# State in 1 KB rows, half of the first x in fp32 by hardware queues, identity transposes ahead of early matmuls, and softmax and w2 work moved to GpSimd

## The chip, the cores and the metric

The kernel runs on one core of a Trainium2 chip. Its engines work side by side: TensorE (PE in the profile, its weight loads PEld), VectorE (DVE), ScalarE (ACT), GpSimd (POOL) and SyncE (SP), which here only issues transfers. The metric is the time of one execution on the device in microseconds (us); lower is better.

## The reference

Two stages follow each other. The first is a cross attention between tokens and a small state, in both directions; the second sends every row through all eight experts, weighted by a matrix that Sinkhorn iterations make.

```python
# x: (8, 8, 512, 64), state: (8, 8, 32, 64)
scores = scale * x @ state^T;   a  = softmax(scores);   xread = a @ state
scores2 = scale * state @ x^T;  a2 = softmax(scores2);  sread = a2 @ x
x = concat([xread, sread], axis=2) -> (4352, 512)       # B*S rows, H*D columns
P = exp(x @ w_gate - max)                               # (4352, 8)
for _ in range(8):
    P /= P.sum(1) + 1e-9;  P /= P.sum(0) + 1e-9;  P *= N / E
for e in range(8):                                      # w1: (512, 1024), w2: (1024, 512)
    out += P[:, e:e+1] * (relu(x @ w1[e]) @ w2[e])
```

## The kernel before

The attention is cut into 16 units, (b, q): batch b and half q of its heads, four heads each. For a unit, x (`x_nat`, cast to fp16 by GpSimd's software queue while it is loaded) is transposed to `xT`: for b < 2 by TensorE (line 578), for the others by a transposing DMA on SP's queue (line 591). `psB` holds the scores of both directions, made of `xT` and the transposed state `stT` (line 605). From there two chains go:

- the token softmax (names with A): DVE turns the scores into `eA`, takes the maximum, subtracts it (`subA`, line 648), ACT takes the exponential, DVE the sum and its reciprocal, DVE or POOL normalizes (`normA`, line 670), and DVE transposes the result to `aT`. The two units of batch 0 (`TOK = 2`) take their scores from TensorE in the token layout instead (`psA`, with `stD`, a spread copy of `stT`), and are transposed back by TensorE (`aT_ps`);
- the state softmax (names with B): maximum on DVE, exponential `E` with its row sum on ACT, reciprocal on DVE, scaling by it (`normB`, line 662) on POOL or DVE, a transposing DMA to `ETs`, and products `su_ps` with `x_nat` (line 758), which also set x buffers free.

xread is never formed. The state is multiplied into the weights first: `V = state @ w1` (`project`, `v_ps`, line 870), and the hidden layer of a batch is `hps = V^T aT` (line 897), then relu. The second layer is `yps` (line 935) for expert 0, and a scheme with fewer products (seven instead of eight, with sums of hidden rows `sm` and of weights `T`) for experts 1 to 7 (`layer1`, `layer2`, lines 255 and 334). The sums `T` of w2 of expert 1 are eight DVE subtractions (line 965) in the stretch of the Sinkhorn iterations.

Three things overlap in the first 134 us: the 16 attention units, expert 0 block by block as units become ready, and, after the last gate, eight Sinkhorn iterations on DVE, each with one column sum on TensorE (`csb_ps`, line 846). Products of expert 0 fill TensorE meanwhile. From 134 us on come experts 1 to 7, issued by loops; `layer2_last` computes the last 256 rows and stores them with eight transfers of 64 KB, alternating between SP's and ACT's queues (line 317).

The order of everything before expert 1 is written out by hand: the program makes a list of operations, each with the engines it may run on, and `PLAN` names number and engine of one after another, as in `662P` or `648A` (P is TensorE, V DVE, A ACT, G POOL, S SP's queue, H the host). Each engine runs its own in that order; the costs in the code beside an operation, such as `{"PE": (0.44, 0.62)}`, are not used by `issue`.

At the start, state is loaded by SP and ACT in two transfers (line 441) of 256 KB each, in rows of 256 bytes, cast and doubled to `st_in` by two engines, and transposed to `stT` by TensorE (line 492). POOL's queue loads x, then the halves of w1 and w2 of expert 0 (lines 468, 545, 548).

Of the kernel before, what the change touches and what calls it, by code (L numbers as in the profile page):

```python
# [12 lines left out]
ALU = mybir.AluOpType  # L13
# [3 lines left out]
6G 0S 1S 2V 7H 44V 3A 33V 32A 34A 8G 56P 36P 35V 55H 37V 10H 45V 57A 42P 58V 9G 38P 40P 43A 59P 4S 39A 41V 5V  # L17
46V 62P 50H 51G 61A 71V 63P 60A 52G 64V 11G 72V 73A 80P 65V 12G 435P 401P 66A 81V 13H 79P 14G 82V 436A 88V
437A 404P 83A 67V 402A 137H 403A 89V 96H 97P 100P 84V 406A 68V 90A 98A 15G 85V 69P 86P 53G 405A 99V 87V 70A
103P 101A 102A 91V 409P 16H 92G 413P 104V 407P 410A 411P 105V 111A 438P 120P 414V 408A 419P 421P 106V 415P  # L20
112V 138S 121V 74V 439A 412A 422V 113V 417P 107A 54G 440A 75G 122V 432P 429P 123V 370V 420A 469P 128A 418A
416A 17G 108V 140P 124A 125V 423P 426P 471A 433P 114A 148V 93S 129V 430P 149V 172H 424P 76S 434A 115V 470A
109G 130V 139S 110V 126G 141V 131A 427P 18G 127V 142V 428V 431A 445P 143V 132V 94P 150A 95V 77P 425A 156P 116G
447P 151V 133V 78V 449P 446A 443P 441P 144A 455P 164V 152G 448A 117S 19H 450V 157V 444A 165V 173S 442A 451P
456A 166A 134S 20G 452A 453P 463P 158V 472P 207H 145V 175P 159V 183V 184V 457P 31G 146G 454A 176V 473A 160A
464P 185A 174S 460P 458P 461P 465A 147V 161V 21G 153S 177V 191P 47P 162G 474A 118P 167V 459A 154P 462A 178V
163V 135P 49A 168G 199V 22H 48V 179A 466P 136A 352P 475P 200V 192V 201A 193V 119V 467P 476A 194V 23G 195A 485P
202V 208S 210P 180V 169S 155A 218V 356P 353A 481P 357V 468A 487P 219V 24G 489P 181G 186V 211V 242H 486A 482A
477P 490V 488A 483P 479P 220A 170P 478A 503P 187G 480A 484V 171A 203G 196V 537P 209S 25H 212V 226P 197G 504A
505A 506P 213V 500P 182V 198V 26G 234V 221V 507A 222V 204S 188S 491P 27G 538A 227V 539A 501P 497P 502A 508A  # L30
492P 235V 243S 228V 244S 214A 229V 511P 215V 236A 523P 230A 498P 494P 216G 245P 495P 515P 512V 499A 277H 231V
524A 493A 517P 246V 253V 223S 496A 247V 521P 516A 237V 254V 519P 509P 522V 518A 248V 513P 232G 189P 520A 255A
205P 510V 224P 514V 540P 28H 278S 261P 249A 190V 269V 29G 225A 270V 262V 531P 534P 206V 238G 250V 532P 256V
358P 271A 535P 217V 541A 533A 233V 542A 312H 279S 263V 272V 536A 354P 280P 528P 543P 529P 525P 288V 289V 251G
555P 264V 281V 265A 282V 239S 257V 526P 359A 266V 544A 530V 556A 545P 355A 547P 549P 273G 553P 527A 546V 571P
313S 290A 548A 283V 605P 550A 554V 296P 267G 606V 304V 572A 305V 240P 573A 557P 284A 607A 558A 551P 297V 552A
568P 360P 258S 241V 285V 30G 291V 306A 559P 562P 574P 298V 252V 315P 299V 286V 569P 576A 268V 323V 563P 575A
274S 300A 560P 570A 292G 316V 361A 561A 581P 564A 307V 565P 362P 324V 317V 301V 325A 302G 566P 363V 582A 326V
579P 587P 583P 287V 314S 588V 591P 567A 580A 639P 608P 584A 592A 347H 303V 331P 577P 348G 641V 640A 610A 609A
339V 293S 589P 585P 275P 332V 259P 578A 327G 586A 260A 590A 294P 340V 308G 333V 341A 593P 309S 318V 319A 334V  # L40
295V 364P 594P 276V 328S 625P 619P 342V 595A 335A 365A 599P 320V 602P 343V 336V 600P 337V 603P 626A 321G 322V
329P 310P 350G 344S 601A 349G 311A 620V 345P 338V 346V 604V 366P 596P 330A 368P 369V 351G 597P 367A 371V 611P
372P 598A 695H 615P 617P 373V 612V 374P 375V 613P 614V 616A 623P 618A 621P 696H 711H 376A 705P 377V 642P 624A
622A 706A 707A 630P 643V 697V 708P 644A 378P 379V 631P 710A 627P 698V 380V 647P 632A 709A 636P 628P 381P 633P
699V 648V 637P 382V 634P 657P 629A 638A 383V 700V 653P 658A 655P 384P 651P 635A 701V 654A 725P 385V 723P 386V
702V 656A 726A 716P 652A 724A 717A 645P 659P 649P 714P 646A 650A 660A 387P 721P 715A 712P 727P 687P 722A 388V
728A 688A 667P 713A 664P 389V 390P 703V 665P 668P 391V 673P 674A 392V 661P 670P 669A 729V 393P 671P 394V 666A
662P 672A 677P 395V 718P 663A 678A 679P 675P 683P 719A 681P 720V 680A 676A 685P 396P 684A 682A 397V 686A 692P
704V 689P 693P 690P 730P 398V 694A 399P 733P 731V 691A 732A 735A 734A 400V
""".split()  # L50
ENGINES = {"P": "PE", "V": "DVE", "A": "ACT", "G": "POOL", "D": "DMA", "S": "SPQ", "H": "HOST"}
NT_ = 2
ETX = 0
POOLB = 1
# [50 lines left out]
def issue(ops):  # L105
    for step in PLAN:
        op = ops[int(step[:-1])]
        assert all(d.end for d in op.after) and ENGINES[step[-1]] in op.on
        for slot in op.takes:
            slot.ring.taken.append(slot)  # L110
            slot.tile = slot.make()
        op.emit(ENGINES[step[-1]])
        op.end = True
    assert all(op.end for op in ops) and len(PLAN) == len(ops)
# [3 lines left out]
def kernel(  # L118
# [180 lines left out]
    def layer2_last():  # L299
# [5 lines left out]
        for row in range(tn // 128):  # L305
# [10 lines left out]
            for i in range(nb):  # L316
                (nc.scalar if i % 2 else nc.sync).dma_start(
                    out=outs[row * nb + i], in_=acc[ds(i * Ns, Ns), k, :])
# [116 lines left out]
    st_in = spl.tile([128, B, NQ, 2, D], FP16, name="st_in")  # L435
    st_st = spl.tile([128, B, NQ, D], FP32, name="st_st")
    loads = []
    for g in range(2):
        def load(g=g):
            bs = ds(g * B // 2, B // 2)  # L440
            (nc.scalar if g else nc.sync).dma_start(
                out=st_st[:, bs], in_=state[bs].rearrange("b (q h) n d -> (h n) b q d", q=NQ))

        loads.append(dma((0, 0), 1.0, load, lands=2.7))
        ops[-1].since, ops[-1].hard = 0.5, 1
# [5 lines left out]
    wgd = dma((0, 2), 0.1, lambda: nc.sync.dma_start(  # L451
        out=wg_st, in_=moe_w_gate.rearrange("(kc p) e -> p kc e", p=128)))
    wgc = op((15.0,), {"DVE": (0.15, 0.25)}, lambda _: nc.vector.tensor_copy(out=wgh, in_=wg_st), [wgd])
    wgc.since = 20.0
# [7 lines left out]
    for b in range(B):  # L462
        x_ready.append([])
        part("x%d" % b)
        got = op((0, 1 + 2 * b), {"HOST": (0.0, 0.0)}, lambda _: None, takes=[xn[b]])
        for g in range(2):
            def load(b=b, g=g):
                nc.gpsimd.dma_start(
                    out=xn[b].tile[:, ds(g * 4, 4), :],
                    in_=x[b, ds(g * 4, 4), :, :].rearrange("h (p sc) d -> p h (sc d)", sc=NSC))  # L470

            x_ready[b].append(dma((0, 1 + 2 * b, g), 1.28 if b else 2.3 - 0.6 * g, load, [got], [], [xn[b]], "POOL"))
            ops[-1].since, ops[-1].hard = 0.7, 1
# [4 lines left out]
    bd = []  # L478
    for g in range(2):
        for s_ in range(2):  # L480
            def place(eng, g=g, s_=s_):
                bs = ds(g * B // 2, B // 2)
                copy(eng, st_in[:, bs, :, s_, :], st_st[:, bs])

            bd.append(op((0, 0, g), {"DVE": (0.50, 0.64)} if s_ else {"ACT": (0.50, 0.65)}, place, loads[g:g + 1] + warmed))
    stT_ready = []
    for g in range(4):
        ps = psum([128, 4, 128], FP16, "stT_ps")

        def turn(_, g=g, ps=ps):  # L490
            for i in range(4):
                nc.tensor.transpose(ps.tile[:, i], st_in[:, 2 * g + i // 2, i % 2].rearrange("p s d -> p (s d)"),
                                    identh)

        def keep(eng, g=g, ps=ps):
            copy(eng, stT[:, ds(2 * g, 2)].rearrange("p b q c -> p (b q) c"), ps.tile)

        t = op((0, 1, g), {"PE": (0.35, 0.55)}, turn, bd[g // 2 * 2:g // 2 * 2 + 2] + [makeh], [ps])
        stT_ready.append(op((0, 1, g), EVICT16, keep, [t], uses=[ps]))
    ND = (TOK + 1) // 2  # L500
    stD_ready = {}
    if TOK:
        stD = spl.tile([128, ND, NQ, 4, 2, Ns], FP16, name="stD")
        zd = op((0, 0, 0), {"POOL": (0.40, 0.50), "DVE": (0.25, 0.35)}, lambda eng: engines[eng].memset(stD, 0.0))
        for b in range(ND):
            def spread(eng, s_, b=b):
# [4 lines left out]
                               lambda eng, s_=s_, spread=spread: spread(eng, s_), stT_ready[b // 2:b // 2 + 1] + [zd])  # L511
# [55 lines left out]
    for b in range(B):  # L567
# [4 lines left out]
                  [x_ready[b][0]], [xT])  # L572
        for g in range(2 if b < NT else 0):
# [11 lines left out]
            t = op((due_x(2 * b + g) - 2.0, 0), {"PE": (0.70, 0.88)}, turnX, [x_ready[b][g], makeh], [ps], [xn[b]])  # L585
# [3 lines left out]
        for g in range(0 if b < NT else 2):  # L589
# [5 lines left out]
            xt_ready.append([dma((due_x(2 * b - 2), 0, g), 2.0, turn, [x_ready[b][g], gotT], [], [xn[b], xT], lands=0.8)])  # L595
            ops[-1].moves, ops[-1].xbar = (3.0, 0.8), 1
            ops[-1].on = {"SPQ": (1.4, 4.5)}
        for q in range(NQ):
# [18 lines left out]
            o2 = op((due_x(2 * b + q), 0), {"PE": (0.13, 0.38)}, score, xt_ready[q] + stT_ready,  # L617
# [490 lines left out]
```

## Time and profile before

| | |
|---|---|
| median of 3 runs | 754.57 us (753.24 to 755.26) |
| the profiled execution | 753.05 us |
| its span, first to last instruction | 751.3 us |
| mean granted TensorE clock | 0.997 |
| start of the first hidden product of expert 0 | 18.66 us |
| start of the first product of expert 1 | 134.45 us |
| end of the last accumulation on DVE | 747.81 us |

In the profile, a line of a group or of the rows in order of time names the line of the kernel, the engine, the operation, what it writes and reads (out<-in), the shapes, and how often; idle time of the engine ahead of it stands in brackets, with what ended it. The mean of a matmul's duration includes its way through the array, so eight in a row take less than eight times the mean. The chain of waits goes back from the last instruction to what released it, step by step. The clock is given as a share of full speed.

### The profile page before, as it was taken

Reading aid. Unit: us, or ns where it says so; the run is one execution under the profiler, and the core shown is the slowest. Engines: PE = TensorE matmul, PEld = TensorE weight load, DVE = VectorE, ACT = ScalarE, POOL = GpSimd, SP = SyncE. Lnnn points to the kernel's source line nnn. Section 1 sums busy time; section 2 is a strip of 40 time slices with the busy share of each in tenths; the row PEclk is TensorE's granted clock in tenths of the full one; section 3 lists DMA queues with packets and bytes.
Section 4 is the critical chain, followed back from the end, with each engine's and each line's share of the span. In section 5 each row is a group of like instructions: output and inputs, shape, how many; then the busy total and the mean of one; then the engine's idle time right before and its main releaser. Section 6 shows DMA issues by size and latency. Waiting matters only on the chain.

```text
span 751.3 us, 16144 instructions
## 1 busy us (share of the span) xinstructions
PE 734.7 (98%) x6517; PEld 501.2 (67%) x6517; DVE 616.3 (82%) x1529; ACT 518.2 (69%) x1014; POOL 70.8 (9%) x81
## 2 busy tenths in 40 slices
PE   4999999999999999999999999999999999999997
PEld 3444445667677777777777677776777777776776
DVE  5999989888888789788887888887897888878875
ACT  6876846798976766666666766667667666676662
POOL 3664310200010000100000000100001000000000
PEclk9999999999999999999999999999999999999999
DMA  9997560600032000600006000330006000002234
GB/s 175 151 133 127 86 92 1 113 2 1 1 66 48 2 1 2 113 1 1 2 4 110 2 1 1 58 56 1 1 2 112 2 1 2 1 29 101 98 113 141
DMA packets 51323, 36.71 MB, mean 49 GB/s; under 512 B 25392, under 2 KB 43824, under 8 KB 51248
## 3 DMA queue, kind: packets, MB, share of 16 engines
q0 software_dynamic: 22272, 20.97, 18.4%
q1 hardware_dynamic: 27744, 14.18, 7.7%
q8 instruction: 51, 0.84, 0.5%
q10 hardware_dynamic: 1232, 0.52, 0.3%
q14 instruction: 24, 0.20, 0.1%
HBM read 42.48 MB, written 8.91 MB: 68 GB/s over the span
## 4 chain that ended last, share of the span: by engine, by line
PE 91%; DVE 3%; DMA 2%; ACT 1%; POOL 1%; issue 0%; SPq 0%; POOLq 0%; ACTq 0%
PE hps L255 28%; PE Bseed L334 20%; PE A L334 14%; PE E L334 13%; PE yps L935 6%; PE v_ps L235 4%; PE hps L897 4%; DMA xT<-x_nat 2%; DMA x_nat<-in_x_dram 1%; DVE acc L348 1%; ACT Hm L275 1%; PE su_ps L758 0%; PE y L312 0%; PE v_ps L870 0%; POOL E L662 0%; ACT V L419 0%
## 5 line engine op out<-in xcount | busy, mean ns | idle before, releaser
L275 ACT ACTIVATE Hm<-hps 128x512 f16<-128x512 f32 (+1 forms) x496 | 265.2, 577 | 128.1 <-PE hps L255 125.3
L255 PE MATMUL hps<-aT,V 128*128 128x512 f16 x880 | 230.1, 379 | 0.0
L334 PEld LDWEIGHTS <-Hm 128*128 128x128 f16 x1888 | 181.4, 98 | 71.2 <-issue 15.8
L348 DVE SCALAR_TENSOR_TENSOR acc<-Bseed,Pmat,acc 128x256 f32<-128x256 f32 x354 | 155.0, 477 | 9.4 <-PE Bseed L334 6.6
L334 PEld LDWEIGHTS <-sm 128*128 128x128 f16 x1416 | 138.2, 98 | 34.1 <-issue 0.4
L334 PE MATMUL A<-w2h,Hm 128*128 128x256 f16 x944 | 123.7, 273 | 0.0
L334 PE MATMUL Bseed<-T,Hm 128*128 128x256 f16 x944 | 123.3, 273 | 0.0
L255 PEld LDWEIGHTS <-V 128*128 128x128 f16 x880 | 86.1, 98 | 51.3
L348 DVE SCALAR_TENSOR_TENSOR acc<-E,Pmat,acc 128x256 f32<-128x256 f32 x236 | 103.1, 476 | 12.5 <-PE E L334 12.5
L281 DVE TENSOR_TENSOR sm<-Hm 128x512 f16<-128x512 f16 (+1 forms) x122 | 50.1, 411 | 64.2 <-ACT Hm L275 64.0
L243 ACT CAST V<-v_ps 128x512 f16<-128x512 f32 x150 | 77.7, 611 | 0.0
L348 DVE SCALAR_TENSOR_TENSOR acc<-A,Pmat,acc 128x256 f32<-128x256 f32 x118 | 51.9, 479 | 17.2 <-PE A L334 16.7
L935 PE MATMUL yps<-w2h,hT 128*128 128x512 f16 x272 | 64.1, 379 | 0.0
L363 ACT COPY Bseed<-A 128x512 f32<-128x512 f32 (+1 forms) x62 | 34.1, 550 | 43.3 <-PE A L334 42.1
L334 PE MATMUL E<-T,sm 128*128 128x256 f16 x472 | 61.7, 273 | 0.0
L334 PE MATMUL E<-w2h,sm 128*128 128x256 f16 x472 | 61.7, 273 | 0.0
L334 PE MATMUL Bseed<-T,sm 128*128 128x256 f16 x472 | 61.5, 272 | 0.0
L282 DVE TENSOR_TENSOR Hm<-Hm 128x512 f16<-128x512 f16 (+1 forms) x122 | 50.2, 412 | 4.2
L284 DVE TENSOR_TENSOR sm<-Hm,sm 128x512 f16<-128x512 f16 (+1 forms) x122 | 50.2, 412 | 4.2
L283 DVE TENSOR_TENSOR sm<-sm,Hm 128x512 f16<-128x512 f16 (+1 forms) x122 | 49.4, 405 | 0.0
L194 POOL DMA_DIRECT2D w1h<-in_moe_w_dram x12 | 8.5, 714 | 397.9 <-PE hps L255 397.4
L935 PEld LDWEIGHTS <-hT 128*128 128x128 f16 x272 | 25.4, 99 | 28.8 <-issue 1.7
(127 smaller groups left out, 609.7 us busy)
## 6 DMA issues: line engine op xcount, KB each, us to landing
w1h<-in_moe_w_dram POOLq DMA_DIRECT2D x16, 512.0 KB, 7.0
w2h<-in_moe_w_dram POOLq DMA_DIRECT2D x16, 512.0 KB, 8.1
out_dram<-acc SPq DMA_DIRECT2D x32, 256.0 KB, 2.6
x_nat<-in_x_dram POOLq DMA_DIRECT2D x16, 256.0 KB, 5.6
st_st<-in_state_dram ACTq DMA_DIRECT2D x1, 256.0 KB, 4.9
st_st<-in_state_dram SPq DMA_DIRECT2D x1, 256.0 KB, 4.3
ETs<-E SPq DMA_TRANSPOSE x16, 3.9
out_dram<-acc SPq DMA_DIRECT2D x4, 64.0 KB, 1.7
```

Source lines behind the costliest of these rows:

```text
L235: nc.tensor.matmul(ps[q][ds(j * Ns, Ns), :], stT[ds(r, 64), bi, q, ds((j ^ q) * Ns, Ns)], w1h[ds(r, 64), 2 * q + j // 2, cols], tile_posit ...
L243: nc.scalar.copy(out=dst, in_=src)
L255: nc.tensor.matmul(out, lhs, rhs, start=(k == 0), stop=(k == len(terms) - 1))
L275: nc.scalar.activation(out=Hm[:, i, j, :tn], in_=hps[:, :tn], func=AF.Relu)
L281: nc.vector.tensor_add(s1, a21, a22)
L282: nc.vector.tensor_sub(a21, a11, a21)
L283: nc.vector.tensor_sub(s2, s1, a11)
L284: nc.vector.tensor_sub(s4, a12, s2)
L334: nc.tensor.matmul(dst[:, c], lhs(j, c), rhs[:, j], start=first and c == 0 and j == 0, stop=(j == NJ - 1), skip_group_check=True)
L348: nc.vector.scalar_tensor_tensor(out=dst, in0=src[:, c], scalar=p[:, k], in1=dst, op0=ALU.mult, op1=ALU.add)
L363: nc.scalar.copy(out=Bb[:, :nk], in_=A[:, :nk])
L935: nc.tensor.matmul(yps.tile, hT[fb].tile[:, ds(tk * 128, 128)], w2h[:, fb, :], start=(fb == 0), stop=(fb == NFB - 1))
```

## The change

The edit has these parts:

1. `state` is read as rows of 1 KB (four state rows of 64 floats side by side in a partition), 128 KB first and then 384 KB in one transfer, both by SP. Four casts with a broadcast make `st_in`, one for each two batches, alternating between engines; the copy out of `stT_ps` puts the columns back in order. Users of `stT` wait for the quarter that they read, not for all four.
2. Heads 0 to 3 of batch 0 are loaded as fp32 by SP and ACT, 256 KB each, into a part of `acc` that is not in use yet, and cast to `x_nat` by DVE and ACT. POOL's software queue loads heads 4 to 7 and all other batches. `wg_st` is loaded later.
3. `IDLE` names seven operations of TensorE ahead of which 2 to 24 transposes (or products) of the identity with itself are issued, 72 in all, into the PSUM tile that the operation then overwrites.
4. `subA` and the sums `T` of expert 1 may run on POOL; `normB` on POOL is a product of two tensors, with the reciprocal broadcast, instead of a tensor times a scalar.
5. `layer2_last` stores its two row tiles with one transfer (256 KB, SP) and two (128 KB each, SP and ACT).
6. `PLAN` is another order of the same operations, with other engines for some. In it ten of the 14 subtractions of `subA` are on POOL (none before), 13 of 16 scalings `normB` (12 before), 9 of 16 normalizations (12 before), and four of the eight sums `T`. Nothing is edited in the loops of experts 1 to 7.

```diff
@@ issue @@
-def issue(ops):
+def issue(ops, idle):
     for step in PLAN:
...
+        idle(op.takes[0].tile if op.takes else None, IDLE.get(int(step[:-1]), 0))
         op.emit(ENGINES[step[-1]])
...
+IDLE = {34: 24, 59: 2, 62: 5, 404: 9, 106: 24, 407: 6, 37: 2}
...
+    def idle(t, n):
+        if not n:
+            return
...
+        for _ in range(n):
+            if t.dtype == FP16:
+                nc.tensor.transpose(t, identh, identh)
+            else:
+                nc.tensor.matmul(t, identh, identh, start=True, stop=True, skip_group_check=True)
@@ layer2_last @@
-            for i in range(nb):
-                (nc.scalar if i % 2 else nc.sync).dma_start(
-                    out=outs[row * nb + i], in_=acc[ds(i * Ns, Ns), k, :])
+                (nc.scalar if c else nc.sync).dma_start(
+                    out=outs[ds(row * nb, nb), :, cols], in_=acc[:, k, cols])
@@ the loads of state and x @@
-            (nc.scalar if g else nc.sync).dma_start(
-                out=st_st[:, bs], in_=state[bs].rearrange("b (q h) n d -> (h n) b q d", q=NQ))
+    st_rows = state.rearrange("b h (k l) d -> (b h k) (l d)", l=4).rearrange("(g p) c -> p g c", p=128)
+    xs = acc[:, ds(0, 2 * XH), :].rearrange("p (g t) d -> p g (t d)", t=2)
...
+        return begin("SPQ", lambda: nc.sync.dma_start(out=st_st[:, a:b], in_=st_rows[:, a:b]), 0.35 * (b - a))
...
+        q = nc.scalar if k else nc.sync
+        return begin("ACT" if k else "SPQ", lambda: q.dma_start(
+            out=xs[:, g, ds(k * 512, 512)].rearrange("p (h c) -> p h c", h=2),
+            in_=x[0, ds(4 * g + 2 * k, 2)].rearrange("h (p sc) d -> p h (sc d)", sc=NSC)), 0.68)
+    loads = load_st(0, 1)
+    xs_in = [[load_x(g, k) for k in range(2)] for g in range(XH)]
+    loads += load_st(1, B // 2) * 3
...
+                    copy(eng, xn[0].tile[:, ds(4 * g + 2 * k, 2), :].rearrange("p h c -> p (h c)"),
+                         xs[:, g, ds(k * 512, 512)])
@@ state to stT @@
+            copy(eng, st_in[:, g], st_st[:, g].rearrange("p (l d) -> p l d", d=D).unsqueeze(2)
+                 .broadcast_to((128, 4, 2, D)))
...
-            copy(eng, stT[:, ds(2 * g, 2)].rearrange("p b q c -> p (b q) c"), ps.tile)
+            copy(eng, stT[:, ds(2 * g, 2)].rearrange("p b q (m l) -> p (b q m) l", l=4), ps.tile.rearrange("p (l m) -> p m l", l=4))
@@ softmax and sums @@
-                engines[eng].tensor_scalar(out=E2.tile, in0=E2.tile, scalar1=rrec.tile, scalar2=None,
-                                           op0=ALU.mult)
+                if eng == "POOL":
+                    nc.gpsimd.tensor_mul(E2.tile, E2.tile, rrec.tile.broadcast_to((128, S)))
+                else:
+                    nc.vector.tensor_scalar(out=E2.tile, in0=E2.tile, scalar1=rrec.tile, scalar2=None, op0=ALU.mult)
...
-                s1 = op(r(4), {"DVE": (0.60, 0.80)}, subA, [m1], [], [eA, mxA])
+                s1 = op(r(4), {"DVE": (0.60, 0.80), "POOL": (1.05, 1.20)}, subA, [m1], [], [eA, mxA])
...
-        nc.vector.tensor_sub(T[:, i, jj], p[:, jj], q[:, jj])
+        engines[eng].tensor_sub(T[:, i, jj], p[:, jj], q[:, jj])
```

## The prediction

> **What bounds the kernel now.** I read the page first, then the busy time by stretch, then the rows of TensorE (PE) in order of time, then the rows of the softmax tiles. The page:
>
> ```profile
> span 751.3 us, 16144 instructions
> ...
> PE 734.7 (98%) x6517; PEld 501.2 (67%) x6517; DVE 616.3 (82%) x1529; ACT 518.2 (69%) x1014; POOL 70.8 (9%) x81
> ...
> PE 91%; DVE 3%; DMA 2%; ACT 1%; POOL 1%; issue 0%; SPq 0%; POOLq 0%; ACTq 0%
> ```
>
> PE sets the time, so only microseconds in which PE waits or runs slowly can be gained. The busy time by stretch says where those are:
>
> ```profile
> core 0: us, PE busy (x) PEld busy (x) DVE busy (x) ACT busy (x) POOL busy (x), PEclk, DMA share, GB/s
> 0.00:7.00 7.00, 0.02 (x1) 0.02 (x2) 1.47 (x4) 2.64 (x4) 6.25 (x14) 1.00 0.88 137
> 7.00:15.00 8.00, 6.18 (x91) 4.60 (x92) 5.98 (x14) 5.49 (x12) 1.26 (x2) 1.00 1.30 197
> 15.00:20.00 5.00, 3.97 (x36) 2.17 (x35) 4.62 (x12) 4.87 (x12) 1.04 (x1) 0.68 1.38 201
> 20.00:100.00 80.00, 77.76 (x883) 36.59 (x882) 73.21 (x165) 60.89 (x137) 42.86 (x41) 1.00 0.84 122
> 100.00:134.40 34.40, 34.13 (x216) 17.21 (x213) 30.64 (x84) 21.71 (x45) 0.00 (x0) 1.00 0.19 32
> 134.40:747.00 612.60, 612.38 (x5305) 440.61 (x5298) 499.89 (x1252) 422.63 (x808) 19.35 (x25) 1.00 0.17 36
> 747.00:751.30 4.30, 0.29 (x3) 0.01 (x1) 0.48 (x1) 0.00 (x0) 0.00 (x0) 0.93 0.49 122
> ```
>
> Experts 1 to 7 (134.4 to 747) have no PE idle time and are not edited. What can be won lies in the first 20 us, in 2.2 us of idle time between 20 and 100, and behind 747. PE's own rows:
>
> ```profile
> 6.98 1.04 PE L578 MATMUL xT_ps<-identh,x_nat 128*128 128x128 f16 x8 [6.98 <-DMA x_nat<-in_x_dram]
> 18.66 2.65 PE L897 MATMUL hps<-aT,V 128*128 128x512 f16 x8
> 37.42 0.30 PE L605 MATMUL psB<-xT,stT 64*32 64x256 f16 x8 [0.76 <-DMA xT<-x_nat]
> 51.64 0.30 PE L605 MATMUL psB<-xT,stT 64*32 64x256 f16 x8 [0.51 <-DMA xT<-x_nat]
> 60.10 0.30 PE L605 MATMUL psB<-xT,stT 64*32 64x256 f16 x8 [0.94 <-DMA xT<-x_nat]
> 73.72 1.89 PE L897 MATMUL hps<-aT,V 128*128 128x512 f16 x8
> ```
>
> PE's first work waits for x until 6.98; expert 0's first hidden product (hps) starts at 18.66, and from there PE is nearly full. Its first eight matmuls take 2.65 us, the same eight at 73.72 take 1.89: the granted clock of 15 to 20 is 0.68. So the measure of the change is when hps starts, and at which clock.
>
> **The change, part by part.** *Work of PE.* From the first hps to the first product of expert 1 (A, at 134.45) both programs hold the same matmuls: 144 hps of 512 columns, 272 yps, 32 hps of 256, and so on. What starts earlier ends earlier, if waits stay alike.
>
> *Start.* hps needs aT of both units of batch 0, and before that a chain over ACT and DVE. In the changed program ACT has in order: cast of x0, one stT copy, two st_in casts, an stD copy, two xT copies, two stT copies, expB, expA, an xT copy, expA. The two casts wait for the last three quarters of state. Loads of before took 4.3 and 4.9 us for 256 KB in 256 B rows, stores of 64 KB in 2 KB rows 1.7. 384 KB in 1 KB rows, issued third on SP at about 1.7, I put at 4.1 us: landed at 5.8 (4.8 to 7.5). From there by rows of before: two casts 1.15, stD 0.35 (a guess between the DVE's 0.22 and an ACT copy's 0.58), two copies 1.07, two copies 1.07, expB 0.69 + 0.19, expA 0.62, copy 0.58, expA 0.62: 12.2. Then DVE: sum and reciprocal 0.85, two normalizations 1.22, one transpose 0.70 which stands ahead, two aT copies 0.80: hps at about 15.8, so **2.9 us** earlier (1.2 to 3.9 from the landing's bounds). The software queue is not later than that: of the first x0 only one half is left on it; its transfers followed each other every 1.3 us for 256 KB (x) and 2.5 us for 512 KB (weights). From x0's second half at 6.5 (6.1 to 7.9; the first one took 5.50 behind half as much hardware traffic), the x1 half that PE needs just before hps lands at 6.5 + 1.3 + 2.5 + 2.5 + 1.3 = 14.1, and the first half of w2 (two x halves ahead of it before, now one less) at about 18, before yps needs it at 15.8 + 4.
>
> *Casts on DVE and ACT* of x0 (0.6 each) replace part of the software queue's conversion; they lie ahead of 5.8 and are hidden by the state's landing. If that comes at 4.8, they stand on the chain with 0.6.
>
> *72 identity transposes*, all but two ahead of the xT and v_ps work: 24 from 1.4 on (106 ns each at the early rate of 8 in 0.85: 2.5 us, over by 4.0, when state has not been cast), the rest 48 between 5 and 14, where PE had 1.8 us of idle time and waits for xT copies, w1 and x1. At 56 ns each (eight weight loads in 0.45 at 14.84) they cost 2.7 us of PE that is not on the chain; should the second 24 stand ahead of ready work, 1.3 us. I count nothing for them. Their return is the clock: 2.65 - 1.89 = **0.76 us** at the first hps. The Trainium skill ("TensorE: Matmul & The Clock Gate", Part 1) says the rate is set by busy time in free-running windows of about 3.4 us; by it, fillers in parts of a window might not hold the rate, and the sum would be without the 0.76. The dip in the 15 to 20 row followed a stretch with 1.8 us idle, which is in its favour, and the fillers stand in that stretch; I keep 0.76 (0 to 1.0).
>
> *20 to 100.* To the maximum of the logits, DVE loses ten eA subtractions (0.68), one E scaling (0.34), two stT, two stD and four small copies (2.1 together), and gains three normalizations (0.69), two V, one aT, one acc, one hT eviction (3.1 together) and others: 3.3 us less of 73. POOL had 12 E scalings of 1.57 and 12 normalizations of 1.05, together 31.4 us; now it has 32 operations, at 1.05 33.6:
>
> ```profile
> L662 POOL TENSOR_SCALAR E<-E,rrec x12: 1553/1564/1990, 19.0 to 88.7; 128x512 f16<-128x512 f16 x12
> ...
> L670 POOL TENSOR_TENSOR a<-eA,rA x12: 1037/1047/1294, 26.2 to 93.7; 128x512 f16<-128x512 f32 x12
> ```
>
> E times a broadcast column is no row of before. It is a two-tensor operation like the second line, so 1.05; at the first line's 1.57 the 13 add 6.8 us to a POOL that is 54% busy. A subtraction that goes from 0.68 on DVE to 1.05 on POOL lengthens one unit's chain by 0.4, and E behind it waits as long; units overlap, so I take the PE waits of this stretch as they are, zero gain (gain 2.2, loss 4).
>
> *Sums of w2:* 8 of 0.41 on DVE become 4 there and 4 on POOL, in the stretch of the Sinkhorn iterations, where one DVE iteration is about 3.7 against 4.05 us of PE work between two column sums: hidden, zero.
>
> *Tail.* Each of the last two row tiles goes out in one or two DMAs instead of four. The last acc write ends at 747.81, two issues follow on ACT to 748.70. One issue (0.49) saves 0.3, but 128 KB in 1 KB rows land later than 64 KB (1.7 to 2.6): **0.1** (-0.3 to 0.3).
>
> Sum: 2.9 + 0.76 + 0.1 = 3.7 us. The profiled execution took 753.05 (span 751.3, 1.75 around it); it goes to 749.3, span 747.6. The median of before is 754.57, 1.5 above the profiled one, so I give 754.57 - 3.7 = 750.9. About 0.3% (2.3 us) is what a measurement can tell from no change.
>
> **Rivals.** *(a) The start does not move.* All loads share 16 DMA engines, already at 1.3 in the row of 7 to 15, and 256 KB of x0 come as twice the bytes. Should state's remainder land at 7.5 or the x1 half after 16, only clock and tail are left: 753.7. Against it: the hardware loads have 1 KB rows now, four times as long. 0.14.
>
> *(b) A lock between DVE and POOL in the Sinkhorn stretch.* DVE rows beside POOL work are at times long:
>
> ```profile
> L648 DVE TENSOR_TENSOR eA<-eA,mxA x14: 627/682/1189, 21.1 to 91.2; 128x512 f32<-128x512 f32 x14
> ```
>
> The 1189 stands at 51.55, in a POOL normalization of 51.15. The four w2 sums on POOL, 1.05 each, can each hold a Pmat product: 4 x 1.05 less four times the slack of 0.4 is 2.6: 753.5. The Trainium skill ("SBUF — State Buffer", "SBUF: two separate sides") states this as an exclusive lock between GpSimd and DVE operations with two SBUF inputs; the long row agrees. In the softmax the same lock should ease, since DVE keeps 11 such operations of 18. 0.06.
>
> *(c) Waits between 20 and 100 vanish* with DVE's 3.3 us: 2.2 to 2.5 more, 748.4. 0.10.
>
> *(d) Slower: POOL's own order.* x loads are issued by POOL and wait for PE to free an x buffer: one wait before was 4.3 us, at 64.89, with an E scaling behind it. Now subtractions, which every unit's chain to the gates needs, queue behind such loads. One stall of 4.3 on the chain gives 755.2, two give 759.5; it decides from 6.0 us of added waits on. Against it: the loads would have to wait as PE runs earlier, and PE's su products that free them run earlier too. 0.10.
>
> **Numbers.** The forecast has 0.60; nine tenths of it lie beyond 0.3%. Faster: 0.54 + 0.10 of (c) = 0.64. Within 0.3%: 0.06 + 0.14 + 0.06, less 0.01 of (a) that could be slower: 0.25. Slower: (d) and that rest, 0.11. The range goes from (c) with the early landing, 747.4, to (d) with one stall, 755.4.
>
> **What would show it.** Right: first hps of aT and V at 15 to 16.7 with eight in about 1.9, a clock of 1.00 in 15 to 20, first A at 130 to 131.5, the same PE rows behind it. Wrong: first hps after 17.5 (a); A later although hps came early, with PE waiting for xT or scores and POOL busy or stuck at a load (d); PE waiting at the column sums of Sinkhorn beside POOL's w2 sums (b). E scalings on POOL at 1.5 would falsify the 1.05.

## The result, and the profile after

The changed kernel takes 762.79 us (median of 4 runs, 761.88 to 763.88) against 754.56 us before (753.24 to 755.26): ratio 1.0112, interval 1.0092 to 1.0131. It is 8.2 us slower; 3.7 us faster was forecast. The profiled execution took 763.88 us, the longest of the four. Its page, in the lines that answer to those of before (span, busy time, the chain of waits by engine):

```profile
span 762.1 us, 16288 instructions
...
PE 740.6 (97%) x6589; PEld 506.8 (66%) x6589; DVE 616.3 (81%) x1520; ACT 516.0 (68%) x1012; POOL 77.0 (10%) x93
...
PE 85%; DVE 7%; DMA 5%; ACT 1%; issue 1%; POOL 0%; SPq 0%; POOLq 0%; ACTq 0%
```

PE still sets the time, but its share of the chain fell from 91 to 85%, and DMA and DVE took it. The two profiled executions, split at the same three events, show where the 10.85 us between their spans lie (A is the first product of expert 1):

| | before | after | difference |
|---|---|---|---|
| first hps (product of aT and V) | 18.66 | 17.76 | -0.90 |
| from there to the first A (expert 1) | 115.79 | 121.46 | +5.67 |
| from there to the end of the last accumulation | 613.37 | 614.11 | +0.74 |
| from there to the end of the span | 3.44 | 8.78 | +5.34 |

The busy time by stretch (columns as in the prediction), with one stretch ending at the new first A:

```profile
core 0: us, PE busy (x) PEld busy (x) DVE busy (x) ACT busy (x) POOL busy (x), PEclk, DMA share, GB/s
...
7.00:15.00 8.00, 6.84 (x103) 5.94 (x104) 6.63 (x14) 7.07 (x15) 3.27 (x5) 0.79 1.30 200
15.00:20.00 5.00, 4.39 (x57) 2.55 (x57) 3.79 (x10) 3.91 (x9) 1.47 (x2) 1.00 1.29 205
20.00:100.00 80.00, 73.38 (x829) 33.66 (x829) 69.71 (x153) 57.06 (x130) 43.47 (x47) 0.96 0.95 127
100.00:139.20 39.20, 38.71 (x273) 20.27 (x267) 33.71 (x88) 21.71 (x49) 5.58 (x6) 1.00 0.10 14
...
752.00:762.10 10.10, 0.81 (x8) 0.49 (x5) 0.94 (x2) 0.00 (x0) 0.00 (x0) 0.70 0.20 60
```

The dip of the clock at 15 to 20 is gone, but one at 7 to 15 and one inside 20 to 100 have come. In 20 to 100 PE is busy for 73.38 us, not 77.76, and with 829 matmuls, not 883. No engine became the bound: DVE and POOL are at 70 and 43 of 80 us. PE waits. Its rows in order of time name the wait (in brackets, with what ended it):

```profile
17.76 3.63 PE L921 MATMUL hps<-aT,V 128*128 128x512 f16 x16
...
34.81 0.41 PE L627 MATMUL psB<-xT,stT 64*32 64x256 f16 x8 [4.43 <-DMA xT<-x_nat]
35.15 3.60 PE L921 MATMUL hps<-aT,V 128*128 128x512 f16 x8
```

Sixteen hps from 17.76 on take 3.63 us at full clock. Then PE stands for 4.43 us, until a transposing DMA brings `xT`, and the eight hps behind take 3.60 us in place of 1.89: the granted clock is 0.50 from 32.4 to 39.2. So the stall costs 4.43 us, and some 2 us more for 4 us of work at half the clock. Where the transfer was held up is seen in POOL's rows in order of time:

```profile
8.76 1.51 POOL L570 DMA_DIRECT2D w2h<-in_moe_w_dram  x2
18.53 1.05 POOL L670 TENSOR_TENSOR eA<-eA,mxA 128x512 f32<-128x512 f32 x1 [8.26 <-DVE mxA L653]
19.53 0.79 POOL L488 DMA_DIRECT2D x_nat<-in_x_dram  x1
```

The load at 19.53 is x2's second half. Before, POOL issued it at 6.71. Now it stands behind both halves of expert 0's w2 and behind the first subtraction, for which POOL waits 8.26 us (until DVE has the maxima). It lands at 26.78, not at 19.92; its transposing DMA lands 7.87 us later, at 34.67. The tail, in SP's and ACT's rows and in the busy time by stretch (last columns: clock, DMA share, GB/s), first after, then before:

```profile
751.88 1.37 SPq L319 DMA_DIRECT2D out_dram<-acc  x2
...
753.37 1.15 ACTq L319 DMA_DIRECT2D out_dram<-acc  x1
```

```profile
756.00:759.00 3.00, 0.00 (x0) 0.00 (x0) 0.00 (x0) 0.00 (x0) 0.00 (x0) 0.50 0.27 97
```

```profile
748.50:749.50 1.00, 0.00 (x0) 0.00 (x0) 0.00 (x0) 0.00 (x0) 0.00 (x0) 1.00 0.77 195
```

While nothing but the merged stores runs, 0.27 of the 16 DMA engines are busy, about four, at 97 GB/s; the stores of 64 KB kept 0.77 busy at 195 GB/s. The merged transfers' outermost dimension has four blocks. Their size alone is not the reason: the stores just ahead of them in the changed kernel (line 388) are 256 KB each too, with 128 rows outermost, and keep all DMA engines busy at 377 GB/s:

```profile
751.00:752.00 1.00, 1.00 (x12) 0.89 (x11) 0.77 (x2) 0.00 (x0) 0.00 (x0) 1.00 1.02 377
```

### The profile page after: what moved, and what is told of

It reads as the page before. It is cut to its first block, busy times and chain, and to the rows that moved or that the text cites. A ratio compares the mean times of both kernels' runs of the same rounds, so it can differ in the third digit from the quotient of the medians.

```text
span 762.1 us, 16288 instructions
## 1 busy us (share of the span) xinstructions
PE 740.6 (97%) x6589; PEld 506.8 (66%) x6589; DVE 616.3 (81%) x1520; ACT 516.0 (68%) x1012; POOL 77.0 (10%) x93
## 4 chain that ended last, share of the span: by engine, by line
PE 85%; DVE 7%; DMA 5%; ACT 1%; issue 1%; POOL 0%; SPq 0%; POOLq 0%; ACTq 0%
PE hps L258 27%; PE Bseed L336 20%; PE A L336 14%; PE E L336 13%; PE v_ps L238 4%; PE yps L959 3%; PE hps L921 2%; DMA w1h<-in_moe_w_dram 1%; DMA xT<-x_nat 1%; DMA ETs<-E 1%; DMA x_nat<-in_x_dram 1%; DVE acc L350 1%; ACT Hm L278 1%; DMA acc<-in_x_dram 1%; PE y L315 0%
```

## The experiments

Each run is compared with the kernel before on the same chip. The profile is one execution of each; the runs of one kernel spread by 1 to 5 us, in one case by 7, and a stall's cost depends on whether the clock falls with it, so medians and profiles differ by some us (the profiled run of e10 lies 2.2 us above its median, that of e13 2.8). Where PLAN is on one line in a run, line numbers stand 31 lower. All runs but the two with "before + ..." hold the changed kernel's start. "Fillers" are the 72 identity transposes.

| run | median | ratio (interval) | first hps | first hps to first A |
|---|---|---|---|---|
| after | 762.79 | 1.0112 (1.0092-1.0131) | 17.76 | 121.46 |
| e2: before + merged stores | 759.43 | 1.0075 (1.0058-1.0092) | 18.89 | 116.44 |
| e15: before + stores of 32 KB | 754.63 | 1.0012 (1.0001-1.0022) | 18.82 | 116.86 |
| e1: after + old stores | 759.51 | 1.0075 (1.0057-1.0094) | 17.04 | 121.16 |
| e5: e1 + x2 early | 757.75 | 1.0059 (1.0039-1.0079) | 17.15 | 120.93 |
| e4: e5 + w1 early | 760.11 | 1.0083 (1.0068-1.0098) | 17.22 | 123.89 |
| e7: e5 + w2 late | 757.70 | 1.0050 (1.0035-1.0065) | 17.32 | 121.56 |
| e8: e5 + expert 1's w2 late | 756.55 | 1.0031 (1.0019-1.0044) | 17.32 | 118.59 |
| e9: e5, no fillers | 757.50 | 1.0052 (1.0038-1.0066) | 16.56 | 122.76 |
| e10: e5 + subtractions on DVE | 759.76 | 1.0071 (1.0053-1.0089) | 18.20 | 124.62 |
| e17: e8, no fillers | 757.28 | 1.0046 (1.0030-1.0062) | 17.33 | 120.14 |
| e13: start + old order | 754.07 | 1.0011 (0.9994-1.0027) | 17.56 | 120.35 |
| e14: e13, no fillers | 753.08 | 0.9992 (0.9983-1.0001) | 16.59 | 117.67 |
| e16: e14 + w2 whole early | 753.07 | 0.9989 (0.9979-0.9998) | 18.70 | 115.71 |
| e18: e14 + subtractions on POOL | 757.48 | 1.0044 (1.0032-1.0057) | 17.37 | 120.64 |
| e19: e16 + subtractions on POOL | 757.81 | 1.0047 (1.0030-1.0063) | 17.53 | 120.93 |

**The tail.** e1 puts the eight stores back into the changed kernel, e2 puts the merged ones into the kernel before:

```diff
-                (nc.scalar if c else nc.sync).dma_start(
-                    out=outs[ds(row * nb, nb), :, cols], in_=acc[:, k, cols])
+            for i in range(nb):
+                (nc.scalar if i % 2 else nc.sync).dma_start(
+                    out=outs[row * nb + i], in_=acc[ds(i * Ns, Ns), k, :])
```

> The changed kernel with the last 256 rows stored as before: eight transfers of 64 KB, 32 partitions each. In the changed kernel's trace the last accumulation on DVE ends at 753.3 of 762.1, 8.8 us before the end, in the trace of before at 747.8 of 751.3, 3.5 us. Theory A (the form of the three merged stores makes them slow): the end comes 5.3 us nearer, 762.8 - 5.3 = about 757.5 us. Rival (the stores are late because of something else at the end, such as the half clock shown from 756 on, or the issue queue): nothing changes, 762 to 763.

> The kernel before with only the merged stores of the last 256 rows (one transfer of 256 KB, two of 128 KB). Theory A: 754.6 + 5.3 = about 759.9 us. Rival (the form of the stores costs nothing by itself): 754 to 755.

e2 is 5.5 us slower than before by the medians, and its span ends 8.9 us behind the last accumulation (748.65 to 757.56). In e1 the end is back at 3.5 us; its median fell by 3.3 us only, with the same stall in the middle and runs from 757.58 to 760.37. Why the same stores cost 5.5 us in one kernel and 3.3 in the other is open. e15 asks whether the rows of 1 KB are the cause: the last row tile of the kernel before goes out by column halves, each in four transfers of 32 rows.

```diff
-                out=outs[row * nb + i], in_=acc[ds(i * Ns, Ns), k, :])
+                    out=outs[row * nb + i][:, cols], in_=acc[ds(i * Ns, Ns), k, cols])
```

> Edit of the kernel before: the last row tile is stored by column halves in eight transfers of 32 KB with 1 KB rows, each half issued behind its accumulation. Theory T1 (a merged store is slow because its outermost dimension has only four blocks, which keeps 4 of 16 DMA engines busy; a share of 0.25 was seen): here every transfer has 32 rows outermost, the share behind the last accumulation is over 0.6, the span ends 2.9 to 3.7 us behind the last accumulation, ratio 0.999 to 1.001. Theory T2 (rows of 1 KB or small transfers are slow by themselves): the span ends 4.5 us or more behind it, ratio 1.0015 or more.

```profile
749.00:750.00 1.00, 0.00 (x0) 0.00 (x0) 0.02 (x1) 0.00 (x0) 0.00 (x0) 1.00 0.85 237
```

With 32 rows outermost and the same rows of 1 KB, 0.85 of the DMA engines work at 237 GB/s, and the span ends 3.9 us behind the last accumulation (expected 2.9 to 3.7; the last tile now has eight issues, not four). T2 falls; T1 holds, though the ratio of 1.0012 is a little over its 1.001: in the profile the rest lies ahead of the first A, in a longer stretch of half clock near 20. The Trainium skill ("DMA: Bandwidth & Descriptors", "Why a DMA increments its semaphore by 16 and not by 1") says that a transfer runs on the largest number of engines up to 16 that divides the slowest dimension of both of its sides: four here, as the share of 0.27 shows.

**The held-up loads.** In POOL's part of PLAN, 15G and 16G load x2's halves, 56G and 57G expert 0's w2, 54G and 55G its w1; 109G is the first subtraction, 49G the copy `stD`, 95G and 78G the first E scalings, 353G and 354G the loads of expert 1's w2, 352G the last one of its w1. e5 moves one load, e4 one more:

```diff
-54G 49G 55G 13G 15G 56G 57G 109G 16G 78G 95G
+54G 49G 55G 13G 15G 16G 56G 57G 109G 78G 95G    # e5
+54G 55G 49G 13G 15G 16G 56G 57G 109G 78G 95G    # e4
```

> The changed kernel with the old stores, and with the load of the second half of x of batch 2 moved in POOL's order from behind the first eA subtraction to right behind the first half, ahead of the loads of w2. In the changed kernel's trace PE waits 4.43 us at 34.81 for the transposed copy of that half (load issued at 19.53, landed at 26.78, transposed copy at 34.67), and the eight hps matmuls behind it take 3.60 us instead of 1.89. Theory B (this one load, moved behind the subtraction and the w2 loads, makes the stall and with it the half clock): the load lands at about 19, stall and slow stretch go, 757.5 - 6.5 = about 751.0 us. Rival (POOL's longer softmax share is the bound, the stall only shows where it bites first): the wait comes back at later units, 755 to 757.5.

> As the kernel with old stores and the moved x load, and with the issue of the second half of w1 on POOL ahead of the stD copy instead of behind it. In the changed kernel's trace that copy waits until 6.11 on POOL, the load is issued at 6.56 and lands at 15.57, 3.9 us behind the first half, and PE waits for it at 15.61 with the aT transposes behind. Theory C (the copy on POOL holds up the load and the first hps): the load lands at about 14.1, the first hps starts about 1.4 earlier than 17.76, 1.4 us below the kernel with the moved x load alone, about 749.6. Rival (the software queue is full anyway, its order of issue does not matter): the same as with the moved x load alone, within 0.5.

Both fell short. e5 has x2 whole at 18.83, yet PE waits as before, only earlier, for less long (2.81 us) and for another `xT`; e7 then issues w2's second half behind the subtraction 109G. PE's rows of e5, then of e7:

```profile
26.96 0.37 PE L596 MATMUL psB<-xT,stT 64*32 64x256 f16 x8 [2.81 <-DMA xT<-x_nat]
```

```profile
26.73 5.52 PE L928 MATMUL yps<-w2h,hT 128*128 128x512 f16 x17 [2.40 <-DMA w2h<-in_moe_w_dram]
```

In e5 the transposing DMA was issued at 17.48 and landed at 26.92, beside software-queue loads that ran until 24.48; in e7, with w2's second half issued later, it took 5.23 us, not 9.44. In e4 w1's second half landed at 14.31 and the first hps stayed at 17.22; besides, half clock fell on the wait of 2.59 us at 93.

> Base: the changed kernel with the eight 64 KB stores and x2's second half loaded right behind its first (ratio to before 1.0059). Edit: the load of w2's second half goes behind the first subtraction on GpSimd, as late as in the kernel before. Theory D (the software queue's loads hold up the transposing DMAs, so that PE waits and its clock halves): the wait of 2.8 us near 27 us and the half clock behind it (1.7 us lost) go; yps may wait up to 1.7 us for w2. Time from first hps to first A 118 to 119 in place of 120.9, ratio about 1.0030. Rival P (GpSimd's share of the softmax holds the chain whatever the loads do): the wait comes back elsewhere, 120.5 to 121, ratio 1.0055 to 1.0065.

e7 takes PE's wait for xT away and gets one for w2: the loads only change places, and neither theory's figure for the wait is met (ratio 1.0050, between the two). In the first 25 us the transfers set the pace. Two more edits of e5:

```diff
-353G ... 351G ... 354G ... 352G
+351G ... 352G 353G 354G                         # e8
-IDLE = {34: 24, 59: 2, 62: 5, 404: 9, 106: 24, 407: 6, 37: 2}
+IDLE = {}                                       # e9
```

> Base as in the run before. Edit: the two loads of expert 1's w2 are issued behind both loads of its w1, so about 5 to 10 us later. Theory D: the transposing DMAs of the last unit then have the DMA engines for themselves, the PE wait of 2.4 us near 93 us falls below 0.8, the time from first hps to first A is 119 in place of 120.9, ratio 1.0035 to 1.0045; the sums of w2 on GpSimd and DVE still end before they are needed. Rival P: the wait stays over 1.5 us, since scores come late from GpSimd; ratio unchanged at 1.0055 to 1.0065.

> Base as in the runs before. Edit: the 72 identity transposes are left out. As predicted blind: they lie off the chain and only hold the clock: first hps at the same time within 0.3 us, its first eight matmuls 2.6 in place of 1.9 us, ratio 1.0065 to 1.0070. Rival I (they delay the work of PE's first 15 us): first hps 1 us or more earlier, ratio 1.0045 or less.

e8 hits: in e5 an ETs transposing DMA issued at 83.64 beside expert 1's weights landed at 91.79 (8.15 us), and PE waited 2.39 us at 93.21; in e8 the same DMA takes 4.07 us and no wait over 0.25 us is left between 85 and 100. The ratio falls by 0.0028, 2.1 us. In e9, without the fillers, the first hps comes 0.6 us earlier; the ratio moves by less than the intervals, and the first hps run at full clock (twelve in 2.76 us), against the forecast of 2.6 us for eight. Other runs without fillers differ in this, see below.

> Base as in the runs before. Edit: the ten subtractions of the token softmax go back from GpSimd to DVE, each in the same place of the order. Theory D: DVE, at 70 of 80 us, gets 6.8 us more and GpSimd's queue is freed of the waits for DVE's maxima, so x loads behind them go out earlier; the waits near 27 and 93 us stay, since neither is a wait for a subtraction; first hps to first A 120.5 to 122, ratio 1.005 to 1.008. Rival P (subtractions on GpSimd hold the chain to the gates and the x loads behind them): time from first hps to first A falls to 118 or less, ratio 1.002 or less.

```diff
-109G 126G 146G 162G 197G 251G 267G 286G 302G 337G
+109V 126V 146V 162V 197V 251V 267V 286V 302V 337V
```

Giving the subtractions back to DVE in the new order makes nothing better: 1.0071, as theory D had it, and the stretch from first hps to first A is longer than either had (124.62, with half clock near 95, in the slowest of its six runs). Why is open; the order around them is laid out for POOL. So the parts had to be tried on the old order.

**The start alone, on the old order.** e13 keeps the new PLAN up to the first hps (91 of its first 97 entries) and lists everything else in the order and on the engines of the kernel before (x2 whole ahead of w2); e14 sets `IDLE = {}` besides.

> Edit: the changed kernel's start (state and x0 loads, casts, fillers, everything ahead of the first hidden product in its order), and behind that the order and the engines of the kernel before for all that remains: its subtractions and sums of w2 on DVE, its order of loads (x2 whole ahead of w2, w2's second half behind the first E scaling, expert 1's w1 ahead of its w2), its eight 64 KB stores. Theory D (the start is worth a little over 1 us and the loss lies in the new order of 20 to 100 us): first hps at 17.0 to 17.8, first A 115.5 to 116.5 later, ratio 0.997 to 1.000. Rival S (an earlier start by itself turns into waits, since transfers set the pace until 30 us): first A 117 or more behind the first hps, ratio 1.000 to 1.004.

> The kernel of the run before without the 72 identity transposes. From the earlier run without them: first hps 0.6 us earlier than with them, at 16.4 to 17.2. If they keep the clock up (as predicted blind), the first eight hps or the work just ahead take 0.7 to 1.7 us longer and nothing is gained: ratio as the run before within 0.001. If they only cost PE time, ratio 0.0008 below the run before.

e13 is level with before, nearer to rival S than to theory D: its 120.35 holds a wait of 2.04 us for w2 and one of 1.76 for an `xT`, with half clock behind the first. Against e1, which has the same stores, it is faster by 0.0064 of the time, 4.8 us: so much the new order behind the first hps costs, its other engines included.

e14 is at 0.9992, further below e13 than either case expected. What the fillers do to the time is not settled: leaving them out changed the ratio by -0.0019 here (1.4 us), by -0.0007 from e5 to e9 and by +0.0015 from e8 to e17, and the intervals overlap each time. What they do to the clock shows in the profiles. In all eight profiles with fillers the first eight hps run at full clock, in 1.90 us. Of the six without, three have this (e9, e14, e17); in e16, e18 and e19 a step of half clock reaches into these hps, and they take 2.25 to 2.65 us. With the start of the kernel before (before, e2, e15) it is 2.65 to 3.57. PE's order is the same in e14 and e18 up to there, and so is the landing of w1 (13.86 and 13.87); the row of e14, then of e18:

```profile
16.59 1.90 PE L890 MATMUL hps<-aT,V 128*128 128x512 f16 x8
```

```profile
17.37 2.65 PE L890 MATMUL hps<-aT,V 128*128 128x512 f16 x8
```

These eight end at 18.5 us in e9 and e14, at 18.9 to 20.1 with fillers, and at 19.2 to 21.0 in the other four without (20.1 in e10 and 21.0 in e16, whose loads came late). This speaks for the fillers' hold on the clock at the start; with one profile of each kernel it is no proof. What they may cost is seen in the transfers between 13 and 14.5 us. In e13 the queue that brings instructions has a packet there (columns: packets, MB, share of the engines); e14 has none:

```profile
q8 instruction: 1, 0.02, 4.0%
```

This packet of 16 KB takes 0.96 us at 13.31 in e13 and 13.52 in the changed kernel, in the midst of the load of w1's second half, which lands at 15.37 and 15.57. In all six profiles without fillers, and in that of before, the packet comes at 17.5 to 18.8 us; w1 lands at 13.8 to 13.9 in five of those six (15.04 in e16, where all loads came late). PE has v_ps of this half ahead of the transposes of `a`: they start at 16.10 in e13, at 14.73 in e14, though DVE's normalizations end together (15.30 and 15.27). That the fillers' instructions pull the packet forward is inferred from these times. The Trainium skill ("Runtime: NRT & Kernel Launch", "Terms") gives 16 KiB blocks for the refill of instruction memory, which fits the packet's size. In e1 and e5 the packet came as early (13.32 and 13.44) and x1's second half was late instead (16.0 and 16.1, 15.2 in e14).

**Subtractions on POOL alone.**

```diff
 # order of e14
-... 95G 57G 78G ... 109V ...
+... 95G 109G 57G 78G ...                         # e18, and the other nine as in e10
 # e16: 57G ahead of 95G;  e19: e16 with e18's subtractions
```

> Base as in the first of these runs (ratio 0.9992, first hps to first A 117.7). Edit: the ten token-softmax subtractions go from DVE to GpSimd, each at its place in the order, with nothing else moved. As predicted blind they cost nothing: ratio 0.998 to 1.000. Rival P (GpSimd waits for DVE's maxima with x loads and scalings queued behind it): x loads are issued later, PE waits for xT, first hps to first A 119 or more, ratio 1.001 or more.

> Base: the changed start without identity transposes, and behind it the order of the kernel before (ratio 0.9992). Edit: the load of w2's second half is issued ahead of the first E scaling on GpSimd, not behind it. Theory D (loads wait in GpSimd's program order, and one that lands late stops PE): w2's second half lands at 24 to 25 us, yps no longer waits for it (1.5 us), first hps to first A 116 to 117, ratio 0.997 to 0.998. Rival S (the DMA engines are full until 30 us, so each load that comes earlier makes a transposing DMA later): a wait for xT of 1 us or more takes its place before 40 us, ratio 0.999 or more.

> The run with w2's second half ahead of the first E scaling (ratio 0.9989, first hps to first A 115.7) with the ten subtractions on GpSimd, each at its place. In the run with subtractions on GpSimd alone (1.0044) GpSimd reached the load of w2's second half 1.2 us later and PE waited 2.6 us for it, with half clock behind it. Theory Q (their price is what is queued behind them): with that load ahead of them the wait is gone, first hps to first A 115.5 to 117, ratio 0.998 to 1.001. Theory L (a subtraction of 1.05 in place of 0.68 us and its turn on GpSimd lengthen the units' own chains): first hps to first A 118.5 or more, ratio 1.003 or more.

POOL's rows of e18, and PE's row behind them, show what the prediction had left out:

```profile
19.98 1.04 POOL L654 TENSOR_TENSOR E<-E,rrec 128x512 f16<-128x512 f16 x1 [9.62 <-DVE rrec L650]
20.99 1.04 POOL L639 TENSOR_TENSOR eA<-eA,mxA 128x512 f32<-128x512 f32 x1
21.98 0.81 POOL L539 DMA_DIRECT2D w2h<-in_moe_w_dram  x1
```

```profile
29.14 5.08 PE L928 MATMUL yps<-w2h,hT 128*128 128x512 f16 x15 [2.56 <-DMA w2h<-in_moe_w_dram]
```

The load that PE waits for is issued 1.2 us later than in e14 (20.77), PE waits 2.56 in place of 1.46 us, and a step of half clock follows. By the ratios the ten subtractions cost 3.9 us: rival P, not the zero of the prediction. e16 takes the wait for w2 away by issuing it ahead (landed 24.85, as theory D says, and rival S's wait for xT did not come); first hps to first A is 115.71, as before's 115.79. Its ratio, 0.9989, is less of a gain than D's 0.997 to 0.998. (In its profile the state landed late, at 8.13 and not 6.3, hence the first hps at 18.70; its median is 1.0 us below that of before, and its interval is the only one that lies below 1, by 0.0002. e14's overlaps it, so the gain of the earlier load is shown in the wait, not in the time.) e19 adds the subtractions to that, and theory Q's number fails: PE does not wait for w2, but 3.41 us for an `xT`. DVE's, POOL's, SP's and PE's rows of e19 tell why:

```profile
27.92 0.15 DVE L650 RECIPROCAL rrec<-rowsum 128x1 f32<-128x1 f32 x1
```

```profile
30.67 1.04 POOL L639 TENSOR_TENSOR eA<-eA,mxA 128x512 f32<-128x512 f32 x1 [1.89 <-DVE mxA L622]
31.68 1.03 POOL L654 TENSOR_TENSOR E<-E,rrec 128x512 f16<-128x512 f16 x1
```

```profile
32.73 1.19 SPq L735 DMA_TRANSPOSE ETs<-E  x1
34.10 1.26 SPq L582 DMA_TRANSPOSE xT<-x_nat  x1
```

```profile
40.53 0.30 PE L596 MATMUL psB<-xT,stT 64*32 64x256 f16 x8 [3.41 <-DMA xT<-x_nat]
```

The reciprocal that E needs is there at 28.07. POOL scales E at 31.68, 3.6 us later, since the subtraction ahead of it waits for DVE's maxima; the two belong to different chains. The ETs transposing DMA waits for E, and behind it in SP's order stands the transposing DMA of the next `xT`. In e16 the same scaling started 0.9 us behind its reciprocal (29.15, 30.06), and that `xT` was issued at 32.51 and landed at 37.02; here it is issued 1.6 us later, takes 6.30 in place of 4.51 us and lands at 40.40. So theory L's figures came true, but for the most part not by its mechanism: of 5.0 us of added waits this one is 3.4, paid by what is queued behind on two queues, and not by one load that can be moved. Another 1.15 us, at 25.92, PE waits for ACT's exponential; why is open.

> The changed kernel with all three repairs of the earlier runs: eight 64 KB stores, x2's second half behind its first with expert 1's w2 loads behind its w1 loads, and no identity transposes; its subtractions and w2 sums stay on GpSimd, its order stays otherwise. Theory D: the repairs add up to the ratio of the run with late w2 loads, 1.0031, less 0.0007 to 0.0019 for the transposes: 1.0012 to 1.0024; first hps at 16.6, first A 118 to 119 later. Rival P (what is left is the softmax on GpSimd): the same or more than 1.003.

e17, the changed order with its loads repaired and no fillers, was expected at 1.0012 to 1.0024 and came at 1.0046: repairs do not add up. Its longest waits are for xT (1.45 and 1.34 us) and for V (1.46 us at 105, with the clock halved behind it).

## Why the prediction was wrong

- **What bounds the kernel**: right. PE's waits and its clock explain the middle, the stretch from first hps to first A: waits over 0.25 us are 6.97 us in place of 2.48 (+4.5), half clock costs some 2.0 in place of 0.76, together 5.7 us, and 5.67 were lost.
- **Start, 2.9 us earlier: mis-sized; 0.9 measured.** The sum had the state landed at 5.8, DVE's normalizations ended at about 14.3 and the first hps at 15.8; measured are 6.3, 15.14 and 17.76. What it left out is on PE: the transposes of `a` (0.61 us), and the order ahead of them, where v_ps of w1's second half stands. This half landed at 15.57. Where it landed at 13.86 (e14, without fillers), the first hps came at 16.59, so the late half is worth about 1.2 us and the chain itself 0.8. The forecast of the software queue, "not later than that", was wrong by 1.3 us for x0's half (7.76 against 6.5) and by 2.8 for w1's (15.57 against 12.8 by the same spacing); 1.5 to 1.7 of this came with the early instruction packet.
- **Identity transposes at nothing, with 0.76 us of clock in return: the clock came, the price is open.** With them the first eight hps take 1.90 us in all eight profiles, without them 2.25 to 2.65 in three of six, which is in favour of the mechanism. Whether they cost nothing is not shown: the instruction packet comes earlier with them, and the three comparisons of time go both ways. The gain was lost elsewhere. In the changed kernel 7 to 15 has a clock of 0.79 in spite of them, and the half clock that counts is at 32.4, behind the stall. The granted clock is recorded in steps of 3.41 us, and which of them are halved differs from run to run. The Trainium skill ("TensorE: Matmul & The Clock Gate", Part 1) speaks of free-running windows of that length; the traces agree.
- **20 to 100, zero (gain 2.2, loss 4): the first of two steps that failed.** E behind a subtraction "waits as long" was put down as 0.4 us per chain, hidden by overlap. The subtractions' moves past loads in POOL's order, and E's past SP's queue, were not followed to their users. The stretch from first hps to first A lost 5.67 us in the profiles; e13 against e1 puts 4.8 us on the new order as a whole. On the old order the subtractions alone cost 3.9 us (e18). On the new one e8 puts 2.1 us on the earlier loads of expert 1's w2, but taking the subtractions back gains nothing (e10), and the repairs do not add up (e17). So how the loss divides over the moves of the new order stays open.
- **Prices on POOL: right.** E times a broadcast column takes 1.03 to 1.05 us (one of the 13 took 1.49), the subtraction 1.05:

```profile
L685 POOL TENSOR_TENSOR E<-E,rrec 128x512 f16<-128x512 f16 x13 | 14.0, 1080 | 6.2 <-DVE rrec L681 5.8 <-DVE nsB L666 0.3
...
L670 POOL TENSOR_TENSOR eA<-eA,mxA 128x512 f32<-128x512 f32 x10 | 10.5, 1046 | 16.4 <-DVE mxA L653 16.2
```

  The last figure is the one that was missing: POOL stood 16.4 us ahead of its ten subtractions, 16.2 of them for the maxima.
- **Sums of w2, zero: nearly right.** POOL waits 26.1 us ahead of the second pair of its sums, and nobody needs it; PE's waits at column sums are 0.42 in place of 0.27. A wait of 0.45 us for V at 140.9 is new.
- **Tail, 0.1 us gained: the second step that failed, wrong by 5.4.** 128 KB was taken to land "later than 64 KB (1.7 to 2.6)"; only bytes and row lengths were looked at, not the transfer's outermost dimension. The Trainium skill's rule spoke against this part and was not weighed. Each of the two steps is enough to leave the range, which ended at 755.4: e2, with the merged stores alone, takes 759.43 us, and e1, without them, 759.51.
- **The rivals.** (d) had the right mechanism, POOL's own order, with chance 0.10, but the wrong instance: loads behind subtractions, and E behind them, not subtractions behind loads that wait for x buffers; with the old stores the changed kernel takes 759.5, its price for two stalls, which is luck, as its waits are other ones. No rival held the tail. (a)'s condition came true (x1's second half landed at 16.41, "after 16"); the start moved by 0.9 us, not by nothing, and it was not the end of the matter. What (b) calls a lock shows in DVE's rows (the four subtractions left there have a mean of 0.89 us, where 0.68 was the usual price; the two long ones, 1.16 and 1.05, run beside POOL work) and not at its predicted place, the Sinkhorn stretch. (c) fell: DVE got its 3.5 us back (73.2 to 69.7 busy), and the waits grew.

## What to carry to other kernels

An instruction that moves to another engine moves past everything in that engine's queue: list the loads behind it and, through each released transfer, the next queue's, down to the engine that sets the time. An earlier start is worth only what the transfers behind it allow; here it gave about 1 us at most, with the old order behind it (e14 and e16, ratios 0.9992 and 0.9989). One profile with and one without a part do not show what the part does: e9 and e14 alone would have said that the fillers do nothing for the clock. Merge transfers only if the outermost dimension still divides over all DMA engines.

## What the runs showed of the hardware

- A store with four blocks outermost runs on a quarter of the DMA engines: 97 GB/s against 195 to 237 for 32 rows.
- Stores of 256 KB with 128 rows outermost ran at 377 GB/s and all engines busy, so the size of a transfer was not what slowed the merged ones.
- A transposing DMA takes 2.4 us at the shortest (e5, issued at 90.65 us) and up to 9.5 us beside software-queue loads (e4, at 17.36).
- A wait of PE of 1.5 to 4.4 us can be followed by a halved clock for one or two steps of 3.41 us, which cost up to 2 us more; e17's wait of 1.46 us and e7's of 2.40 were, e19's of 3.41 was not.
- With identity transposes ahead of the first products the clock was full at these in eight profiles of eight; without them in three of six.
- An instruction packet of 16 KB in the load stream takes 0.96 us (e13). With it at 13 to 14 us the load of w1 or of x1 behind it landed about 0.8 to 1.7 us later than in e14; that the packet did this is inferred.
